# Long convolution and soft mixture of experts: the last eleven steps and the end as one list of stages

## The chip, the cores and the metric

The kernel runs on one core of a Trainium2 chip. Its engines work at the same time, each through its own queue in order: TensorE (PE; its weight loads are shown apart as PEld), VectorE (DVE), ScalarE (ACT), GpSimd (POOL), and SyncE (SP), which issues nearly all transfers. All numbers are float32. The metric is the device time of one execution in microseconds, as the median of the runs; lower is better.

## The reference

```python
Xf = np.fft.rfft(x, n=2 * S, axis=1)              # x: (8, 5696, 128), h: (5696, 128)
Hf = np.fft.rfft(h, n=2 * S, axis=0)
y = np.fft.irfft(Xf * Hf[None], n=2 * S, axis=1)[:, :S, :]
x = y.reshape(B * S, D)                           # 45568 tokens of 128
logits = x @ phi                                  # 32 slots, 8 experts of 4
d = np.exp(logits - logits.max(0)); d /= d.sum(0) + 1e-9      # over the tokens
slot_input = d.T @ x                              # (32, 128)
slot_out[e] = np.maximum(slot_input[e] @ w1[e], 0) @ w2[e]    # F = 1024
c = np.exp(logits - logits.max(1)); c /= c.sum(1) + 1e-9      # over the slots
return c @ slot_out
```

## The kernel before

The sequence of 5696 rows is seen as 89 rows of 64 columns, and the convolution is a transform in two stages forward, a product with the spectrum of h, and two stages back. A scratch in device memory lies between the stages. The work comes in three kinds.

- First stage, `stage_a(c, high)`: 72 chunks c (9 sequences, h first, of 8 chunks). `fold(c)` adds and subtracts mirrored columns on POOL (L216); the matmuls stand in L240, ACT takes the two banks out (L242), and two stores go to `fl` (the low columns, each chunk) or `fh` (the high ones, each second chunk, for two chunks at once).
- Middle, units u, 12 for each sequence, 0 to 107: `load_g(u)` loads from `fl` or `fh` (L272; three buffers). `stage_b1(u)` ("forward") multiplies on PE (L285) and then by the spectrum on DVE (L305 twice, L313 twice). `stage_b2(u)` ("backward") multiplies back (L328), ACT takes it out to `zst` (L333; three buffers), and the stores go to `zm` (two of 256 KB) for the first eight units of a sequence or to `zr` (four of 128 KB) for the rest. Forward u and backward u write the same one of two psum tiles, `bt` or `bz` by u % 2, so forward u + 2 waits until ACT has taken backward u out.
- Last stage and the layer of experts, pairs T, 4 for each sequence, 0 to 31: `load_main` and `load_rest` load `zc` (1024 KB) and `zx` (512 KB). `stage_c1` has two parts: the product (L413, L418, into four banks; ACT takes two out, L421 and L422; DVE adds and subtracts one, L405 and L406), and the sums (L405, L406 again, then four operations of L431 on POOL). Then `stage_c2` (turn: transposes, L440, L442), `stage_c3` (logits, L449, L454), `column_max` (L458 to L466), `stage_c4` (exponent: transposes of the logits, L476, L480, and the exponentials over tokens, L483, L487), `stage_c5` (tokens, L492, L495), `softmax_shift` (DVE L501, POOL L502), `softmax_exp` (ACT L508), `dispatch` (16 small matmuls, L533, and the sum on DVE, L538), `softmax_sum` (DVE L513 to L515), `softmax_scale` (POOL L520), and `stage_c6` (weights: transposes, L557; out to a scratch by L567 and L568, or in the end straight into `cT` by L562).

A store is not issued where it is made: it is put on `pending`, and `flush()` issues what is pending. A transfer on SP waits for its own data and for the buffer that it fills, and also for an earlier transfer, because completions share eight semaphores; whatever stands behind it on SP waits too. The banks of psum for everything except the units are four until the last unit is done and eight after that; which of them a stage gets is settled when the program is built.

A loop over 81 steps t sets the order. Up to step 71 each step has first-stage work: `low t` comes first in a step, `high` in each odd step behind the exponent; 1 or 2 units are done in a step (91 and 92 in step 70, 93 in 71, 94 and 95 in 72, and so on to 106 and 107 in step 80), each forward followed by the backward of the unit before it; product and sums of pair T come in step 2T + 27, right behind `low t` while there is one, exponent to exp of pair T in step 2T + 29, dispatch to scale of T in step 2T + 30, turn to maximum in step 2T + 28, weights in step 2T + 32. From step 73 on one of the eight `w1` is loaded at the end of each step (L737).

Behind the loop `front` is closed, which frees the memory of the units, and a list of words, `order`, sets the order of what is left: pairs 27 to 31, the placing of the weights that were put in the scratch (`place`, POOL L578; `cl`, L573), the loads of `w2` (L774), the experts (`inputs`, `hidden`, `flip`, `second`, `outputs`, L794 to L854). Last come the output matmuls (L908), their copies on DVE and ACT (L914, L916) and the stores (L924, L929).

Of the kernel before, what the change touches and what calls it, by code (L numbers as in the profile page):

```python
# [75 lines left out]
def kernel(  # L76
# [145 lines left out]
    def flush():  # L222
        while pending:
            pending.pop(0)()  # L224
# [390 lines left out]
    last_front = queue[-1][1]  # L615
# [19 lines left out]
    for t in range(last_front + 1):  # L635
# [13 lines left out]
        def slot_b(between=lambda: None):  # L649
# [6 lines left out]
            between()  # L656
# [4 lines left out]
        if t < NA:  # L661
            stage_a(t, False)
            fold(t + 1)
        if t == last_front:
            assert T is None and U is None
            assert pair(-1) % NQ
            flush()
            dispatch(W)
            for i in range(3):
                slot_b()  # L670
                flush()
                if i == 1:
                    softmax_sum(W)
                    softmax_scale(W)
                    stage_c2(V)
            assert not us and not wait_b2
            stage_c6(X)
            stage_c3(V)
            column_max(V)
            break  # L680
        if t % 2:
# [7 lines left out]
            if t < NA:  # L689
                slot_b()  # L690
                if U is not None:
                    stage_c4(U)
                stage_a(t, True)
            else:
                slot_b(lambda: stage_c4(U))
# [5 lines left out]
        else:  # L701
            if t % NJ == 0:
                prefetch(wait_b2[-1] + AHEAD if wait_b2 else AHEAD - 1)
            if t < NA:
                load_x(t // 2 + 2)
# [3 lines left out]
            if t < NA:  # L709
                slot_b()  # L710
                if W is not None:
                    softmax_sum(W)
                    softmax_scale(W)
                    dispatch(W)
                flush()
                if V is not None:
                    stage_c2(V)
                if X is not None:
                    stage_c6(X)
                slot_b()  # L720
            else:
                dispatch(W)
                slot_b()
                softmax_sum(W)
                softmax_scale(W)
                stage_c2(V)
                slot_b(lambda: stage_c6(X))
# [233 lines left out]
```

## Time and profile before

| what | value |
|---|---|
| time, median of 3 runs | 838.8 us (835.96 to 839.89) |
| the profiled execution's own time | 839.15 us |
| its span, first to last instruction | 837.4 us |
| mean granted TensorE clock | 0.955 |
| PE busy | 731.3 us (87%) |
| PEld busy | 361.2 us (43%) |
| DVE busy | 595.6 us (71%) |
| ACT busy | 424.6 us (51%) |
| POOL busy | 410.8 us (49%) |
| moved by the transfers | 282.48 MB, mean 337 GB/s |

The busy times are shares of the whole span, over stretches with different limits. For this change one stretch matters: the list begins where `low` of chunk 70 starts on PE, 601.02 us from the start of the span, and ends where the output matmuls start, at 772.38. What follows that, 65 us of output, holds the same instructions before and after.

In the rows of a timeline the first number is the start in us from the start of the span, the second how long the row lasted, then engine, line, operation, the tiles, how many instructions were merged, and in square brackets how long the engine had been idle before it and what ended that. In rows of a list of stretches each engine has its busy time and in brackets its instructions, then the granted clock, the busy share of the 16 transfer engines, and GB/s.

### The profile page before, as it was taken

How to read it: one execution, taken by the hardware profiler on the slowest of the kernel's cores; microseconds unless marked ns; L12 is line 12 of the kernel's file. 1: busy time of each engine (PE TensorE's matmuls, PEld its weight loads, DVE VectorE, ACT ScalarE, POOL GpSimd, SP SyncE). 2: the span in 40 equal slices, each digit the busy share in tenths (PEclk: the TensorE clock that was granted, in tenths of full speed). 3: DMA queues.
4: the chain of work that ended last, by engine and by line, in shares of the span. 5: the costliest groups of instructions: out<-in, count | busy, mean ns of one | idle time of the engine just before them, and what ended most of it. 6: DMA issues, size and time to landing. Idle time of an engine off the chain costs nothing.

```text
span 837.4 us, 21166 instructions
## 1 busy us (share of the span) xinstructions
PE 731.3 (87%) x8308; PEld 361.2 (43%) x8308; DVE 595.6 (71%) x895; ACT 424.6 (51%) x868; POOL 410.8 (49%) x368
## 2 busy tenths in 40 slices
PE   5868788779999999999999999999998887888893
PEld 1222233234444444444444444444444444455783
DVE  0039877747877877777788788777888996794642
ACT  2423344435655555566566555555664544564541
POOL 5634424235665555555555655565533353676000
PEclk9989999989999999999999999999999998999755
DMA  8999999999999999999999999999998995773998
GB/s 291 365 340 372 336 338 358 323 351 398 352 321 371 374 352 330 371 361 349 328 383 360 343 340 370 369 328 342 385 324 258 386 358 192 280 276 103 374 401 341
DMA packets 169707, 282.48 MB, mean 337 GB/s; under 512 B 13352, under 2 KB 132776, under 8 KB 164392
## 3 DMA queue, kind: packets, MB, share of 16 engines
q1 hardware_dynamic: 168600, 280.03, 95.0%
q8 instruction: 66, 1.08, 0.5%
q10 hardware_dynamic: 1008, 1.10, 0.4%
q14 instruction: 33, 0.27, 0.1%
HBM read 148.54 MB, written 132.53 MB: 336 GB/s over the span
## 4 chain that ended last, share of the span: by engine, by line
PE 40%; DMA 27%; ACT 9%; DVE 8%; POOL 6%; issue 4%; SPq 3%; ACTq 0%; DVEq 0%; POOLq 0%
PE bank L240 10%; PE bt L285 6%; DMA zx<-zr 6%; PE bank L413 5%; PE bz L328 5%; DMA zr<-zst 5%; POOL y L431 5%; DMA out_dram<-o 4%; PE bank L418 3%; DMA gt<-fl 3%; ACT zst L333 3%; ACT fst L242 3%; PE bank L449 2%; SPq L224 2%; DMA zm<-zst 2%
## 5 line engine op out<-in xcount | busy, mean ns | idle before, releaser
L240 PE MATMUL bank<-x,s 128*32 128x512 f32 (+1 forms) x1152 | 217.5, 613 | 10.8 <-POOL x L216 8.6
L216 POOL TENSOR_TENSOR x<-xc 128x512 f32<-128x512 f32 x144 | 180.4, 1278 | 88.4 <-PE bank L240 77.3
L431 POOL TENSOR_TENSOR y<-y,op 128x512 f32<-128x512 f32 x64 | 78.2, 1221 | 193.6 <-DVE op L405 191.0
L242 ACT ACTIVATE fst<-bank 128x512 f32<-128x512 f32 x216 | 122.6, 593 | 75.9 <-PE bank L240 48.9
L305 DVE TENSOR_TENSOR pi<-bt,Hi 128x1024 f32<-128x1024 f32 x96 | 112.5, 1172 | 41.7 <-PE bt L285 40.9
L285 PE MATMUL bt<-gt,wt 64*64 64x256 f32 x1620 | 115.7, 394 | 26.8 <-DMA gt<-fl 10.6
L333 ACT ACTIVATE zst<-bz 128x1024 f32<-128x1024 f32 x96 | 93.2, 971 | 85.5 <-PE bz L328 61.1
L313 DVE TENSOR_TENSOR yf<-bt,pi 128x512 f32<-128x512 f32 x192 | 119.2, 662 | 3.3
L305 DVE TENSOR_TENSOR bt<-bt,Hr 128x1024 f32<-128x1024 f32 x96 | 113.0, 1177 | 0.0
L240 PEld LDWEIGHTS bank<-x,s 128*32 128x32 f32 (+1 forms) x1152 | 52.8, 124 | 128.1 <-issue 87.4
L328 PE MATMUL bz<-yf,vt 64*64 64x256 f32 x1440 | 101.7, 385 | 6.8 <-DVE yf L313 6.7
L285 PEld LDWEIGHTS bt<-gt,wt 64*64 64x64 f32 x1620 | 54.3, 134 | 103.6 <-issue 29.1
L405 DVE TENSOR_TENSOR y<-bank,y 128x512 f32<-128x512 f32 x32 | 22.1, 689 | 81.8 <-ACT y L421 81.8
L440 PE MATMUL bank<-ident,y 109*128 109x109 f32 x512 | 64.3, 268 | 17.3 <-ACT yt L442 14.9
L328 PEld LDWEIGHTS bz<-yf,vt 64*64 64x64 f32 x1440 | 55.7, 134 | 34.6 <-DVE yf L313 13.4
L508 ACT ACTIVATE L<-L 128x512 f32<-128x512 f32 x32 | 20.3, 634 | 91.9 <-POOL L L502 91.9
L440 PEld LDWEIGHTS bank<-ident,y 109*128 109x128 f32 x512 | 50.6, 144 | 34.4 <-POOL x L216 20.8
L431 POOL TENSOR_TENSOR y<-y,om 128x512 f32<-128x512 f32 x54 | 64.0, 1186 | 2.1
L520 POOL TENSOR_TENSOR L<-L,rs 128x512 f32<-128x512 f32 x32 | 33.6, 1050 | 61.2 <-DVE rs L515 37.2
L421 ACT ACTIVATE y<-bank 128x512 f32<-128x512 f32 x32 | 19.1, 597 | 79.4 <-PE bank L418 79.4
L413 PE MATMUL bank<-zc,im 64*64 64x512 f32 x480 | 58.5, 602 | 1.0 <-DMA zc<-zm 1.0
L442 ACT ACTIVATE yt<-bank 128x360 f32<-128x360 f32 x128 | 52.8, 485 | 4.8 <-PE bank L440 4.3
(99 smaller groups left out, 834.7 us busy)
## 6 DMA issues: line engine op xcount, KB each, us to landing
fl<-fst SPq DMA_DIRECT2D x144, 256.0 KB, 6.2
gt<-fl SPq DMA_DIRECT2D x72, 512.0 KB, 5.8
zm<-zst SPq DMA_DIRECT2D x128, 256.0 KB, 6.3
zc<-zm SPq DMA_DIRECT2D x30, 1024.0 KB, 8.3
fh<-fst SPq DMA_DIRECT2D x72, 256.0 KB, 7.3
xc<-in_x_dram SPq DMA_DIRECT2D x32, 512.0 KB
out_dram<-o SPq DMA_DIRECT2D x16, 1024.0 KB, 4.7
zx<-zr SPq DMA_DIRECT2D x30, 512.0 KB, 8.3
```

What stands on the lines that cost most here:

```text
L216: nc.gpsimd.tensor_tensor(out=y_[:, o, :, :], in0=near, in1=far, op=AL.subtract if o else AL.add)
L240: nc.tensor.matmul(p[i * m:(i + 1) * m, :], s1[:, q + o, cols], columns(c_, o), start=True, stop=True)
L242: nc.scalar.activation(st[:, :, q, :], p[:, :].rearrange("p (n d) -> p n d", d=D), AF.Copy)
L285: nc.tensor.matmul(bt[q * HP:(q + 1) * HP, a, o, :], wt[r, 2 * i + q, :], t_[r, 2 * o + q, :, :].rearrange("p c d -> p (c d)"), start=True ...
L305: nc.vector.tensor_tensor(out=p_, in0=pv, in1=h_, op=AL.mult)
L313: nc.vector.tensor_tensor(out=y_[r, 0:k, c, :], in0=pv[:, :, c, :], in1=pi[r, 0:k, 1 - c, :], op=op_)
L328: nc.tensor.matmul(bz[a * HP:(a + 1) * HP, q, o, :], vt[r, i, a, :], y_[r, a * m + o, :, :].rearrange("p c d -> p (c d)"), start=True, sto ...
L333: nc.scalar.activation(st[:, 0:m, 0:n, :].rearrange("p o q x -> p q o x"), bz[:, 0:n, 0:m, :], AF.Copy)
L413: nc.tensor.matmul(ps[o, c][h_ * HP:(h_ + 1) * HP, :], im[r, c, :], zt[r, h_, :, c, :], start=True, stop=False)
L431: eng.tensor_tensor(out=part_, in0=part(v, 0), in1=o_[:, :, :], op=sign)
L440: nc.tensor.transpose(p[:, i * TR:(i + 1) * TR], ys[T][0:TR, k * CH + i, 0:D], ident[0:TR, 0:TR])
L442: nc.scalar.activation(yt[:, k * CH:(k + 1) * CH, :, :], of_tokens(p), AF.Copy)
```

## The change

The loop now ends behind step 69. What steps 70 to 80 did, and what the old list `order` did, is written as one list of words that is run in three parts, because `lead` and `front`, pools of memory, are closed between them. Each word is a stage and its number: `low`, `high` and `fold` a chunk, `loadf`, `forward` and `backward` a unit, `load`, `loadz`, `loadr` and the words from `product` to `weights` a pair, `fetchv` one `w1`. The functions behind the words are the same as before; the stages done are the same ones, each once. `load 28`, which stood directly behind `front.close()`, and the last `w1` are words too. The way in which x is loaded (even partitions, and each fourth one) is the same in both.

Steps 70 to 80 before, written in the same words, and the list after, up to the end of the units:

```text
before
 70: low70 fold71 flush forward91 loadf94 backward90 rowsum20 scale20 dispatch20 flush turn21
     weights19 forward92 loadf95 backward91 logits21 maximum21 flush
 71: low71 product22 sums22 flush load23 forward93 backward92 exponent21 high71 tokens21 shift21
     exp21 flush
 72: loadf96 flush dispatch21 forward94 loadf97 backward93 rowsum21 scale21 turn22 forward95
     loadf98 weights20 backward94 logits22 maximum22 flush
 73: product23 sums23 flush loadz24 forward96 loadf99 exponent22 backward95 tokens22 shift22 exp22
     flush fetchv0
 74: loadr24 flush dispatch22 forward97 loadf100 backward96 rowsum22 scale22 turn23 forward98
     loadf101 weights21 backward97 logits23 maximum23 flush fetchv1
 75, 77, 79: product sums flush load forward loadf exponent backward tokens shift exp flush fetchv
 76, 78: dispatch forward loadf backward rowsum scale turn forward loadf weights backward logits
     maximum flush fetchv
 80: flush dispatch25 forward106 backward105 flush forward107 backward106 flush rowsum25 scale25
     turn26 backward107 flush weights24 logits26 maximum26
after
 "flush weights19 low70 fold71 backward90 flush forward91 rowsum20 scale20 dispatch20 "
 "flush turn21 loadf94 forward92 product22 loadf95 backward91 flush logits21 flush "
 "maximum21 sums22 load23 forward93 backward92 exponent21 low71 high71 tokens21 shift21 "
 "flush loadf96 flush forward94 loadf97 backward93 exp21 dispatch21 rowsum21 turn22 "
 "forward95 scale21 weights20 backward94 logits22 maximum22 flush product23 sums23 loadf98 "
 "forward96 backward95 flush loadz24 "
 "loadf99 exponent22 tokens22 shift22 exp22 fetchv0 flush loadr24 flush dispatch22 flush "
 "forward97 loadf100 backward96 rowsum22 turn23 forward98 loadf101 weights21 logits23 "
 "scale22 maximum23 flush backward97 fetchv1 product24 sums24 load25 forward99 exponent23 "
 "backward98 loadf102 flush shift23 tokens23 fetchv2 dispatch23 exp23 forward100 loadf103 "
 "backward99 rowsum23 turn24 forward101 loadf104 product25 backward100 logits24 maximum24 "
 "scale23 weights22 fetchv3 exponent24 sums25 flush load26 forward102 loadf105 backward101 "
 "tokens24 shift24 exp24 fetchv4 flush dispatch24 flush forward103 loadf106 flush "
 "backward102 rowsum24 scale24 turn25 forward104 weights23 flush loadf107 logits25 "
 "maximum25 fetchv5 product26 sums26 backward103 flush loadz27 exponent25 loadr27 flush "
 "forward105 backward104 tokens25 shift25 exp25 flush forward106 backward105 dispatch25 "
 "forward107 backward106 flush rowsum25 flush scale25 turn26 backward107 weights24 "
 "logits26 flush fetchv6 maximum26 "
```

The diff, cut to its core (in the old list `+0` is pair 27):

```diff
-    last_front = queue[-1][1]
+    END = NA - 2
...
-    for t in range(last_front + 1):
+    for t in range(END):
...
-        if t == NA:
-            lead.close()
-            wts = inner.enter_context(tc.tile_pool(name="wts", bufs=1, side="right"))
-            w1s = wts.tile([P, E, F], F32, name="w1s")
-        if NA < t <= NA + E:
-            nc.sync.dma_start(out=w1s[:, t - NA - 1, :], in_=moe_w1[t - NA - 1])
...
+    def run(words):
+        for word in words.split():
+            name, n = re.fullmatch(r"([a-z]+)(\d*)", word).groups()
+            stages[name](*[int(n)] if n else [])
...
+    lead.close()
+    wts = inner.enter_context(tc.tile_pool(name="wts", bufs=1, side="right"))
+    w1s = wts.tile([P, E, F], F32, name="w1s")
...
     front.close()
...
-    load_pair(V + 2)
-    nc.sync.dma_start(out=w1s[:, E - 1, :], in_=moe_w1[E - 1])
...
-    order = (
-        "spread product+0 weights-2 exponent-1 clear shift-1 sums+0 tokens-1 load+2 exp-1 fetch "
-        "fetch dispatch-1 rowsum-1 scale-1 turn+0 logits+0 maximum+0 exponent+0 shift+0 exp+0 "
-        "product+1 place2 sums+1 tokens+0 weights-1 dispatch+0 load+3 zero rowsum+0 scale+0 "
-        "place2 product+2 sums+2 load+4 turn+1 logits+1 product+3 maximum+1 turn+2 exponent+1 "
-        "tokens+1 shift+1 exp+1 sums+3 place2 dispatch+1 rowsum+1 logits+2 weights+0 fetchw0 "
-        "fetchw2 maximum+2 scale+1 exponent+2 shift+2 product+4 turn+3 place2 sums+4 tokens+2 "
-        "exp+2 weights+1 logits+3 dispatch+2 maximum+3 rowsum+2 place2 fetchw4 scale+2 turn+4 "
-        "exponent+3 fetchw6 shift+3 logits+4 tokens+3 exp+3 weights+2 place4 maximum+4 rowsum+3 "
-        "scale+3 exponent+4 dispatch+3 tokens+4 join dispatch+4 shift+4 weights+3 exp+4 inputs "
-        "rowsum+4 scale+4 place32 hidden0 hidden1 flip0 weights+4 flip1 second0 second1 outputs ")
+    run(
+        "load28 product27 exponent26 clear fetchv7 shift26 sums27 flush tokens26 spread weights25 "
+        "load29 exp26 fetch fetch dispatch26 flush rowsum26 turn27 logits27 maximum27 exponent27 "
+        "scale26 weights26 shift27 product28 tokens27 flush place2 sums28 exp27 loadz30 zero "
+        "loadr30 rowsum27 dispatch27 place2 product29 load31 flush turn28 scale27 logits28 sums29 "
+        "product30 maximum28 exponent28 turn29 tokens28 shift28 exp28 sums30 rowsum28 weights27 "
+        "logits29 fetchw0 fetchw2 scale28 maximum29 place2 dispatch28 exponent29 shift29 "
+        "product31 turn30 place2 sums31 tokens29 logits30 exp29 weights28 place2 rowsum29 fetchw4 "
+        "dispatch29 scale29 maximum30 turn31 exponent30 logits31 fetchw6 flush shift30 weights29 "
+        "tokens30 exp30 place4 maximum31 rowsum30 exponent31 dispatch30 tokens31 scale30 join "
+        "dispatch31 shift31 weights30 exp31 inputs rowsum31 scale31 place32 hidden0 hidden1 flip0 "
+        "flip1 second0 second1 weights31 outputs ")
```

More of the change, by code (lines that the diff above doesn't have):

```diff
@@ L660 @@
         T, U, V, W, X = [pair(k) for k in (0, 2, 1, 3, 5)]
[L661 to L680, printed above, removed]
+        stage_a(t, False)
+        fold(t + 1)
         if t % 2:
@@ L688 @@
                     load_rest(pair(-2))
[L689 to L695, printed above, removed]
+            slot_b()
+            if U is not None:
+                stage_c4(U)
+            stage_a(t, True)
             if U is not None:
@@ L753 @@
     y_ = tail["pool"].tile([P, Q * CH, D + 1], F32, name="y2", tag="y2", bufs=1)
[L755 removed]
+    landed = []
     def fetch_c():
@@ L854, in join_experts @@
         nc.vector.tensor_copy(out=so4[:, :], in_=p[:, 0:D])
[L855 to L859 removed]
+    stages.update(place=placed_c, fetchw=load_w2, clear=clear_y, spread=spread, fetch=fetch_c, join=join_quarters,
                   zero=zero_slots, inputs=expert_in, hidden=layer_1, flip=turn_h, second=layer_2,
                   outputs=join_experts)
[L862 removed]
[10 rows of a table removed]
[L873 to L879 removed]
+    run(
[11 rows of a table added]
+    assert not (Ls or ys or ds or prods or gs or zs or xs or folded or kept or landed or held)
     inner.close()
```

54 lines of the change are left out of this document (20 added, 34 removed), and 18 rows, old and new, of tables (scale, w1s).

## The prediction, made before the changed kernel ran

> **What bounds the kernel now.** I read the list of stretches first, to see which engine sets the end where, then the timeline of each stretch for the idle times in brackets.
>
> ```profile
> 600.00:620.00 20.00, 19.29 (x232) 9.38 (x228) 15.91 (x25) 11.72 (x25) 9.13 (x9) 1.00 1.01 347
> 620.00:640.00 20.00, 16.96 (x236) 8.97 (x232) 17.94 (x29) 10.09 (x24) 10.23 (x10) 1.00 0.87 279
> 640.00:660.00 20.00, 17.22 (x232) 9.60 (x232) 19.19 (x29) 10.52 (x21) 8.23 (x8) 1.00 0.93 332
> 700.00:720.00 20.00, 15.35 (x160) 8.13 (x156) 11.20 (x20) 10.96 (x33) 8.62 (x12) 0.91 0.82 311
> 772.00:837.00 65.00, 45.79 (x712) 42.35 (x712) 29.18 (x51) 24.44 (x50) 4.25 (x9) 0.64 0.93 361
> ```
>
> Up to 620 PE is the bound (19.29 of 20 us), with DVE idle for 4.1. From 640 on, without first-stage work, DVE is (19.19). From 700 on, nothing is: the one chain through PE, ACT, DVE and POOL is. From 772 on the stores run at 361 GB/s, and the order of that part is untouched, so it only starts earlier or later. No edit changes an operation; the sum is of idle times.
>
> **The first-stage steps (601 to 633): 0.3 us gained.** The list puts `product22` and `forward93` ahead of `low71`, so that DVE gets its sums sooner:
>
> ```profile
> 611.47 1.94 PE L240 MATMUL bank<-x,s 128*64 128x512 f32 x8
> 617.02 0.69 DVE L405 TENSOR_TENSOR y<-bank,y 128x512 f32<-128x512 f32 x1 [2.51 <-ACT y L421]
> 607.97 0.57 PE L440 MATMUL bank<-ident,y 109*128 109x109 f32 x4 [0.71 <-ACT yt L442]
> 622.05 1.09 PE L533 MATMUL bank<-y,d 128*32 128x129 f32 x32 [0.80 <-ACT d L495]
> 633.44 0.69 DVE L405 TENSOR_TENSOR y<-bank,y 128x512 f32<-128x512 f32 x1 [1.69 <-ACT y L421]
> ```
>
> The 2.51 us before the sums of pair 22 go. But at the next product DVE waits again (1.69 at 633.44), and that wait ends when PE has done the same work as before: between `low70` and `product23` the list holds the same stages. PE's own idle there is 0.71 + 0.80 = 1.51, so no more can be won. The list keeps the first (the fourth transpose still waits for the first copy), saves the second, and adds one: `forward93` needs `zst91`, which now stands on ACT behind the two copies of `product22`, about 0.5. I take 0.3, with bounds of 1.5 gained and 1.5 lost (the clearest loss, a late load, is the rival below). [...]
>
> **The steps on DVE (633 to 694): 0.95 us gained.** DVE's order is nearly the old one. In each pair it stands still once, for ACT's copy of the new product:
>
> ```profile
> 650.13 0.69 DVE L405 TENSOR_TENSOR y<-bank,y 128x512 f32<-128x512 f32 x1 [0.47 <-ACT y L421]
> 666.82 0.69 DVE L405 TENSOR_TENSOR y<-bank,y 128x512 f32<-128x512 f32 x1 [0.47 <-ACT y L421]
> 683.51 0.69 DVE L405 TENSOR_TENSOR y<-bank,y 128x512 f32<-128x512 f32 x1 [0.47 <-ACT y L421]
> 667.67 1.09 PE L328 MATMUL bz<-yf,vt 64*64 64x256 f32 x16
> ```
>
> `product24` keeps its place. `product25` and `product26` now stand before the backward (1.09 on PE, in the row at 667.67 a later one), so their copies come before DVE asks: 2 x 0.47 = 0.94. What stands behind them instead, the backward, has slack: its store's buffer is asked for three units later. Bounds: 0, if another wait takes the place, and 1.41 for all three.
>
> **The change-over (694 to 715): 0.75 us gained.**
>
> ```profile
> 703.40 0.59 PE L557 MATMUL bank<-ident,L 109*128 109x109 f32 x4
> 704.02 0.59 ACT L422 ACTIVATE om<-bank 128x512 f32<-128x512 f32 x1
> 704.85 0.66 ACT L562 ACTIVATE cT<-bank 128x90 f32<-128x90 f32 x4 [0.23 <-DMA zr<-zst]
> 705.36 0.63 ACT L480 ACTIVATE L<-bank 128x512 f32<-128x512 f32 x1
> 706.68 0.66 PE L492 MATMUL bank<-ident,dt 128*128 128x128 f32 x4 [2.25 <-ACT dt L483]
> ```
>
> Before, `weights25` stands between `product27` and `exponent26`, and its copies into `cT` (memory just freed) hold ACT until the last `zr` stores have landed. L480 stands behind them, then L483, then PE's `tokens26`, which waited 2.25. After, the exponent and the tokens come first. L480 then starts at about 704.6, when ACT's copies of the product end (L422, 704.02 + 0.59), instead of 705.36: 0.75, and the chain of dispatch and turn behind it follows. The wait for the stores moves to POOL's `clear`, with `shift26` behind it, which before stood behind `spread` on the same wait. Bounds 0 and 2.25.
>
> **The middle of the end (715 to 750): 0.8 us gained.**
>
> ```profile
> 731.21 1.60 ACT L442 ACTIVATE yt<-bank 128x360 f32<-128x360 f32 x4
> 732.72 0.60 ACT L480 ACTIVATE L<-bank 128x512 f32<-128x512 f32 x1
> 734.04 0.66 PE L492 MATMUL bank<-ident,dt 128*128 128x128 f32 x4 [1.36 <-ACT dt L483]
> 735.38 1.95 PE L533 MATMUL bank<-y,d 128*32 128x129 f32 x32 [0.69 <-ACT d L495]
> ```
>
> PE idles for 1.36 + 0.69 = 2.05 around pair 28. `exponent28` now comes before `turn29` on PE and ACT, and `dispatch28` behind `weights27` and `logits29`, so both waits have work under them. Against it, the four copies of the turn (1.60) now stand on ACT behind L480 (0.60) and the exponentials (about 0.8, as L492 starts 1.32 behind L480's start), so `logits29` can wait up to 1.4 longer for them; but it used to stand behind the dispatch (1.95), which has gone behind it. And `turn28`'s last bank waits for `dispatch27`'s sum, which stands behind the three row sums of pair 27 on DVE, about 1.1. 2.05 - 1.1 = 0.95, of which I take 0.8. Bounds: 2.05 gained, 1.6 lost.
>
> **The last stages: 0.4 us gained.**
>
> ```profile
> 766.05 0.54 PE L557 MATMUL bank<-ident,L 109*128 109x109 f32 x4
> 767.39 3.70 PE L841 MATMUL bank<-w2s,zc 128*32 128x128 f32 x128
> 771.16 0.29 DVE L850 COPY so<-bank 128x128 f32<-128x128 f32 x1 [2.97 <-PE bank L841]
> ```
>
> `weights31` leaves the chain in front of the second layer (0.4 of its 0.54, as transposes start before the last ends) and runs while DVE copies the result (0.29). Its copies into `cT` are needed only by the last batch and by the small tile for the odd row. Bounds 0 and 0.54.
>
> **The clock: 1.4 us gained.**
>
> ```profile
> 692.00:694.00 2.00, 0.65 (x4) 0.20 (x4) 1.97 (x3) 1.14 (x2) 0.00 (x0) 1.00 0.42 161
> 694.00:696.00 2.00, 1.66 (x16) 0.78 (x16) 1.86 (x4) 0.00 (x0) 0.00 (x0) 0.61 0.59 169
> 696.00:700.00 4.00, 4.00 (x32) 3.04 (x32) 1.48 (x5) 3.19 (x7) 1.05 (x1) 0.77 0.30 84
> 708.00:712.00 4.00, 3.98 (x46) 3.53 (x47) 3.93 (x5) 1.42 (x3) 2.56 (x2) 0.57 0.95 358
> 732.00:736.00 4.00, 1.95 (x23) 1.45 (x25) 3.62 (x8) 3.20 (x9) 1.89 (x2) 0.93 0.99 371
> 736.00:740.00 4.00, 3.98 (x48) 2.39 (x43) 3.93 (x5) 1.26 (x7) 3.92 (x4) 0.65 1.00 405
> ```
>
> Each time that PE has idled for 2 us or so (1.35 of 692 to 694, the 2.25 before 706.68, 2.05 of 732 to 736), the granted clock is low for the next 3 to 4. The time lost is busy time by what is missing of the clock: 1.66 x 0.39 + 4.00 x 0.23 = 1.57 behind 693, 3.98 x 0.43 = 1.71 behind 707, 3.98 x 0.35 = 1.39 behind 735; together 4.7. The idle at 734 is the one that the list breaks up most, so I take its 1.4; the one at 707 shrinks less, and the first is only split in two. Bounds 4.7 gained and, for one new spell, 1.5 lost. [...]
>
> **The sum.** 0.3 + 0.95 + 0.75 + 0.8 + 0.4 + 1.4 = 4.6. The profiled execution took 839.15 us (1.75 of it outside its span of 837.4), 0.35 above the median of the runs and inside their range. 839.15 - 4.6 = 834.55; taken from the median it would be 834.2. I forecast 834.3.
>
> **The rivals.** (1) Slower: SP's queue. Where a waiting transfer stands ahead, all behind it is late.
>
> ```profile
> 614.08 1.24 SPq L224 DMA_DIRECT2D fl<-fst x2
> 623.64 4.07 SPq L272 DMA_DIRECT2D gt<-fl x3
> 666.71 0.33 SPq L375 DMA_DIRECT2D zc<-zm x1
> fl<-fst SPq DMA_DIRECT2D x144, 256.0 KB, 6.2
> gt<-fl SPq DMA_DIRECT2D x72, 512.0 KB, 5.8
> gt<-fh SPq DMA_DIRECT2D x27, 512.0 KB, 8.9
> zc<-zm SPq DMA_DIRECT2D x30, 1024.0 KB, 8.3
> ```
>
> `loadf96` must wait for the stores of `low71`. These were issued at 614.08, 9.6 us ahead of it; after, `low71` stands about 6 us later on PE and the stores directly ahead of the load, at about 621 to 622. So it goes out at 622 + 6.2 = 628.2, lands at 634.0, and `forward96` is wanted at about 632. PE waits 1.8; DVE, busy with pair 23 until about 635.9 (four of 0.69 from 633.44, less 0.3), does not feel it up to 0.8 more. If loads there take 8.9, it is 3.1 more and costs 2.3 net, and `loadz24` and all stores behind it slip too. The same again at `loadz26`: the scratch store of `weights22` (now done behind `product25`) stands ahead of it and of two units' stores, so it goes out at about 670 instead of 666.71, with 8.2 left for its 8.3; 3.1 more costs about 2.3. Then the first three terms (2.0) are lost too, with some 1 us for the last loads: 839.15 + 2.3 + 2.3 + 1 + (4.6 - 2.0 taken off) = 842.2, and 846.8 when both spots cost twice that. It decides from landings of about 6.6 us on. For it: the transfer engines are busy for 0.87 to 1.01 of these stretches. Against it: no product of steps 640 to 690 waited for its load. (2) No difference: DVE's work from 633 to 694 and the chains of the end are the same ones, each wait that goes is followed by another, and only the forced parts stay: half of 0.95, 0.75 and 0.4, about 1 us; 838. For it: DVE's order barely changes. (3) More: two of the cold spells go, or all: 834.3 - 1.57 - 1.71 = 831.0. (4) That the change does nothing is out: in the built program the engines' queues stand in the new order from chunk 70 on.
>
> **The numbers.** The forecast (832.6 to 836.5) 0.40, the slower case 0.20, no difference 0.23, more 0.17. A difference under 0.5% (4.2 us, 834.6 to 843.0) is about what cannot be told from none. Faster: somewhat over half of the forecast, all of (3): 0.41. Slower: the upper part of (1): 0.14, with a little for what I have not seen, 0.17. Within: 0.42. The range leaves out about 0.1 at each end: 829.5 to 843.0.
>
> **What would show it.** `sA` of pairs 25 and 26 (L405) without the 0.47; DVE's wait before pair 23's at 1.2 to 1.7; L480 of pair 26 within 1.1 us of the end of `product27`'s last matmul; granted clock over 0.9 where `dispatch28` runs; `weights31` behind the last L841. The distance from `low70` to the output's first matmul, 171.36 before (601.02 to 772.38), should be about 166.8. I am wrong if PE waits for `gt` before `forward96` by over 2.5 us, if `product24` or `product26` waits for `zc`, or if new cold spells stand where PE idled between `forward106` and `forward107`.

## The result, and the profile after

| kernel | median of runs | ratio to the kernel before, 95% interval |
|---|---|---|
| before, beside the changed kernel | 838.29 us (834.05 to 843.93, 20 executions) | |
| changed | 834.94 us (830.3 to 840.2, 20 executions) | 0.9955 [0.9936, 0.9973] |
| changed, a second comparison | 836.92 us (833.91 to 842.74, 12) | 0.9996 [0.9971, 1.0020] |
| before against itself | 839.23 us (835.31 to 844.34, 12) | 1.0003 [0.9973, 1.0033] |

The changed kernel is a little faster: 0.45% in the first comparison, nothing to speak of in the second. Weighted by the inverse squares of the widths of their intervals the two give 0.9970 [0.9955, 0.9985], about 2.5 us; they lie farther apart than such intervals let one expect, so its size is known to 2 us only.

The profiled execution took 839.07 us (span 837.2). It is in the upper part of its 20: its list began 2.76 us later than before (603.78 against 601.02), behind 600 us in which no instruction was moved. So I measure from the start of the list (`weights19`, which now stands ahead of `low70`) to the output's first matmul. The timeline of PE in the changed kernel (start, length, and in brackets the idle time before and what ended it):

```profile
603.78 0.54 PE L557 MATMUL bank<-ident,L 109*128 109x109 f32 x4
...
682.32 1.95 PE L413 MATMUL bank<-zc,im 64*64 64x512 f32 x16 [0.56 <-DMA zc<-zm]
...
706.42 0.66 PE L492 MATMUL bank<-ident,dt 128*128 128x128 f32 x4 [1.75 <-ACT dt L483]
...
725.66 1.87 PE L440 MATMUL bank<-ident,y 109*128 109x109 f32 x16 [1.69 <-POOL y L431]
...
735.48 0.66 PE L492 MATMUL bank<-ident,dt 128*128 128x128 f32 x4 [1.59 <-ACT dt L483]
...
766.74 3.70 PE L839 MATMUL bank<-w2s,zd 128*32 128x128 f32 x128
770.37 0.59 PE L557 MATMUL bank<-ident,L 109*128 109x109 f32 x4
770.86 0.49 PE L850 MATMUL bank<-so,rep 128*128 128x128 f32 x2
771.82 1.52 PE L897 MATMUL op<-so,cT 32*128 32x128 f32 x29 [0.47 <-DVE so L852]
```

771.82 - 603.78 = 168.04, against 171.36: 3.32 gained, of 4.6 predicted. `weights31` (770.37) stands behind the second layer; the wait before pair 26's tokens (L492) fell from 2.25 to 1.75; and `turn28` (725.66) waits 1.69 us for POOL, a wait that was not there before. `tokens28` (735.48) still waits, 1.59 us where it was 1.36, and `product26` (682.32) waits 0.56 for its `zc`: a sign of being wrong that I had named. DVE's timeline, the sums of pairs 23 to 26 (the rows of L405 alone):

```profile
635.71 0.69 DVE L405 TENSOR_TENSOR y<-bank,y 128x512 f32<-128x512 f32 x1 [1.92 <-ACT y L421]
653.22 0.69 DVE L405 TENSOR_TENSOR y<-bank,y 128x512 f32<-128x512 f32 x1 [0.49 <-ACT y L421]
668.54 0.68 DVE L405 TENSOR_TENSOR y<-bank,y 128x512 f32<-128x512 f32 x1
671.04 0.69 DVE L405 TENSOR_TENSOR op<-bank,om 128x512 f32<-128x512 f32 x1 [0.27 <-PE bank L476]
...
686.00 0.69 DVE L405 TENSOR_TENSOR y<-bank,y 128x512 f32<-128x512 f32 x1
```

The waits of pairs 25 and 26 are gone, as predicted; a small one for a bank (0.27) is new. The list of stretches (PE's busy time first, then the granted clock as the third number from the end):

```profile
692.00:696.00 4.00, 2.44 (x52) 1.53 (x52) 3.96 (x6) 1.54 (x2) 2.01 (x2) 1.00 0.99 369
696.00:700.00 4.00, 3.76 (x42) 2.40 (x39) 3.73 (x9) 2.27 (x5) 0.02 (x1) 1.00 0.77 229
704.00:708.00 4.00, 1.94 (x28) 1.49 (x24) 3.17 (x5) 3.21 (x11) 1.27 (x3) 0.99 0.54 165
708.00:712.00 4.00, 3.91 (x47) 3.20 (x40) 3.93 (x5) 1.77 (x6) 3.81 (x5) 0.58 0.85 294
732.00:736.00 4.00, 2.41 (x25) 2.21 (x24) 3.36 (x8) 2.81 (x8) 1.67 (x2) 1.00 0.99 342
736.00:740.00 4.00, 3.63 (x57) 2.17 (x59) 3.93 (x4) 3.25 (x12) 3.12 (x3) 1.00 0.97 367
```

Of the three spells of a low clock, those behind 693 and 735 are gone; the one behind 706 stays. A new one stands at 640 (36 us from the start of the list).

### The profile page after: what moved, and what is told of

It reads as the page before. It is cut to its first block, busy times and chain, and to the rows that moved or that the text cites. A ratio compares the mean times of both kernels' runs of the same rounds, so it can differ in the third digit from the quotient of the medians.

```text
span 837.2 us, 21161 instructions
## 1 busy us (share of the span) xinstructions
PE 728.5 (87%) x8308; PEld 360.6 (43%) x8308; DVE 595.6 (71%) x895; ACT 425.9 (51%) x868; POOL 411.6 (49%) x368
## 4 chain that ended last, share of the span: by engine, by line
PE 41%; DMA 31%; DVE 10%; ACT 8%; SPq 3%; issue 3%; POOL 2%; ACTq 0%; DVEq 0%; POOLq 0%
PE bank L240 11%; DMA zx<-zr 9%; PE bt L285 7%; DMA zc<-zm 6%; PE bank L413 5%; PE bz L328 5%; DMA out_dram<-o 4%; PE bank L418 4%; DMA zr<-zst 3%; ACT fst L242 3%; DMA fl<-fst 3%; SPq L224 2%; ACT zst L333 2%; DMA gt<-fl 2%; DVE pi L305 2%
## 5 line engine op out<-in xcount | busy, mean ns | idle before, releaser
L405 DVE TENSOR_TENSOR y<-bank,y 128x512 f32<-128x512 f32 x32 | 22.1, 690 | 83.0 <-ACT y L421 83.0
L413 PE MATMUL bank<-zc,im 64*64 64x512 f32 x480 | 58.3, 601 | 1.3 <-DMA zc<-zm 1.3
```

Of the source, the lines that this page charges most:

```text
L413: nc.tensor.matmul(ps[o, c][h_ * HP:(h_ + 1) * HP, :], im[r, c, :], zt[r, h_, :, c, :], start=True, stop=False)
```

## The experiments

One profile of a kernel is one draw, so the table sets all of them side by side, cut where the same instruction can be found in each: the start of the list, the first sum (L405) of pair 24, that of pair 26, `tokens26` (L492), `product31` (L413), the output's first matmul. The last column tells where spells of a low clock began, in us from the start, by stretches of 2 us: the first one in which PE's busy time, times what was missing of the clock, was over 0.1 us. Each number is the difference of two rows of a timeline. The ratios in the text are to the kernel before, run beside each: `e1` to `e4` in one batch, `e5` to `e7` beside `a1_changed_again`, `e9` and `n2` beside `b1_before_again`, `n3` by itself, each batch on another chip.

| kernel | start to sums 24 | to sums 26 | to tokens26 | to product31 | to output | in all | low clock at |
|---|---|---|---|---|---|---|---|
| before | 49.11 | 33.38 | 23.17 | 33.14 | 32.56 | 171.36 | 92, 106, 134 |
| b1_before_again | 49.11 | 33.39 | 23.18 | 33.05 | 35.07 | 173.80 | 92, 106, 134, 158 |
| changed | 49.44 | 32.78 | 20.42 | 33.08 | 32.32 | 168.04 | 36, 104 |
| a1_changed_again | 49.66 | 32.78 | 20.42 | 36.17 | 32.34 | 171.37 | 36, 104, 124 |
| e1_steps_only | 50.22 | 32.65 | 22.50 | 35.74 | 35.07 | 176.18 | 106, 126, 136, 160 |
| e2_end_only | 49.12 | 33.38 | 25.20 | 34.43 | 32.35 | 174.48 | 92 (to 103), 112 |
| e3_place_behind | 49.59 | 32.98 | 20.42 | 32.67 | 32.35 | 168.01 | none |
| e4_exponent22_first | 50.66 | 32.65 | 20.42 | 34.98 | 32.30 | 171.01 | 108 |
| e5_loads_later | 49.87 | 32.65 | 20.42 | 31.77 | 32.34 | 167.05 | 88, 102 |
| e6_loads_and_chain | 49.51 | 32.64 | 19.31 | 35.00 | 33.14 | 169.60 | 88, 106 |
| e7_weights25_front | 49.25 | 32.65 | 22.78 | 33.40 | 32.34 | 170.42 | 36, 104 |
| e9_load24_first | 49.17 | 32.64 | 20.42 | 34.71 | 32.33 | 169.27 | 102, 122 |
| n2_all | 48.75 | 32.64 | 20.41 | 31.17 | 33.14 | 166.11 | 102 |
| n3_exponentials_first | 49.25 | 32.64 | 19.93 | 33.20 | 33.78 | 168.80 | 36, 106 |

Most columns repeat to 0.1 us wherever the same words stand there. What scatters is the first column, the spells, and the stretch from `tokens26` to `product31`.

**The two kernels once more.** No edit.

> The changed kernel itself, unaltered, for a second profiled execution. Theory: which of PE's idle times of about 2 us is followed by a low clock differs from one execution to the next, since the kernel without weights moved (the one with only the end's two placings behind) showed none at pair 22 though its list is the same there; so the spell at 640 to 644 is absent or another one appears, and the distance from low70 (with weights19) to the output's first matmul differs from 168.04 us by 1 us or more in either direction. Rival: the spells belong to the order: the same ones at the same places and a distance of 167.6 to 168.5. In both cases the ratio is 0.9940 to 0.9975.

> The kernel before itself, unaltered, for a second profiled execution and for what a comparison of a kernel with itself gives here. Theory: the waits that set off a low clock are the order's, the places where it then falls are partly chance, so of the three spells of the first profile (92, 106 and 134 us behind low70) one or two come again, the distance from low70 to the output's first matmul lies within 3 us of 171.36, and the ratio within 0.997 to 1.003. Rival: the spells come again at the same three places and the distance is 171.0 to 171.8.

The changed kernel took 171.37 where its first profile took 168.04, and its ratio, 0.9996, is above what I expected in either case. Nearly all of that, 3.09, lies between `tokens26` and `product31`. About 1.0 of it comes at `turn27`, which waited for POOL:

```profile
705.79 3.17 PE L440 MATMUL bank<-ident,y 109*128 109x109 f32 x16 [1.06 <-POOL y L431]
```

POOL's first operation in this place, `clear` (L776), does not start before the last `zr` stores have landed, and `shift26` and the sums of pair 27 stand behind it. It came 1.33 behind the start of `tokens26` here (703.04 and 701.71), and 0.06 ahead of it in the first profile. POOL's timeline in `e3`, where the wait for POOL before `turn27` is 1.07, names the stores:

```profile
702.48 0.12 POOL L776 MEMSET y<- 128x16 f32 x1 [6.13 <-DMA zr<-zst]
```

In every profile POOL's first operation behind these stores starts 1.5 us behind the end of their last issue (also in the two of the changed kernel, where the row names ACT as the releaser), 102.2 to 104.2 behind the start of the list; it is 103.9 in the three profiles with the old steps. Of the rest, 0.7 lies at `turn27` and the logits behind it, where the spell at 104 lasted longer (6.8 us at 0.50, and 3.4 in the first profile), and 1.3 at `turn28`: POOL came 1.95 late for it instead of 1.69, and a new spell stood behind it (124). The kernel before shows its three spells again at the same places, and a fourth at 158, which cost 2.5. That one stands in two of the three profiles with the old end (`e1` too, at 160) and in none of the eleven with the new. So the places mostly belong to the order, and which of them is taken differs from one execution to the next (the one at 36 stands in four of ten profiles with the same words, the last section); by the means of two profiles each, 172.6 and 169.7, the change wins 2.9.

**Half of the change at a time.** `e1` has the old end behind the new steps, `e2` the new end behind the old steps:

```diff
 e1   run("... logits26 flush fetchv6 maximum26 ")        # new
-     run("load28 product27 exponent26 clear fetchv7 shift26 sums27 flush tokens26 spread weights25 ...
+     run("load28 fetchv7 spread product27 weights25 exponent26 clear shift26 sums27 tokens26 load29 ...
 e2   the words of steps 70 to 80 before, then the new third list
```

> New order from step 70 to the end of the units, old order for pairs 27 to 31 and the end. Measure: the distance from low70's first matmul to the output's first matmul (171.36 us before, 168.04 after). Theory: the new trace is 2.15 us ahead at product27, most of it because the cold spell of the clock behind step 80 is gone; that lead is kept by the old end, so the distance is 169.0 to 169.7, the ratio to the kernel before about 0.9975. Rival: the old end's weights25 waits on ACT for the last zr stores, which are as late as ever, so the lead is lost at the change-over: 170.8 to 171.4, ratio 0.9990 to 1.0005.

> Old order for steps 70 to 80, new order for what stands behind. Theory: the end by itself wins what the change-over (about 0.9) and weights31 (0.3) won and loses nothing in the middle: 170.0 to 170.4 for the distance, ratio about 0.9985; the cold spell behind step 80 (694 to 700 before) stays, that of 736 to 740 goes. Rival: with the cold spell behind step 80 back, the exponent of pair 26 is late as well and the change-over wins nothing: 171.0 to 171.5. A result under 169.5 would say that the end won most of the change.

The ratios are 0.9983 [0.9957, 1.0008] and 0.9972 [0.9948, 0.9996]; multiplied they give 0.9955, the whole change's in the first comparison, so the times don't show that the halves need each other. What follows rests on the traces. In `e1` the lead is there at `product27`, which starts 97.96 behind the start of the list (696.06 - 598.10) and did so 99.46 behind it before. At `tokens26` it is gone: 105.37 and 105.66. ACT's timeline in `e1`:

```profile
699.60 0.59 ACT L422 ACTIVATE om<-bank 128x512 f32<-128x512 f32 x1
701.64 0.66 ACT L562 ACTIVATE cT<-bank 128x90 f32<-128x90 f32 x4 [1.45 <-DMA zr<-zst]
702.15 0.63 ACT L480 ACTIVATE L<-bank 128x512 f32<-128x512 f32 x1
702.63 0.79 ACT L483 ACTIVATE dt<-lt,low 128x352 f32<-128x352 f32 x2
```

ACT stands for 1.45 until the last `zr` stores have landed, with L480 and L483 queued behind it: the rival's mechanism. (The distance, 176.18, is longer than the rival's: the spells at 126, 136 and 160, and 1.72 of waiting for `zx` of pair 24.) In `e2` (174.48) neither of my numbers came. The clock stayed at about half behind the old steps' last units, and `tokens26` came 2.03 later behind the sums of pair 26 than before:

```profile
692.00:702.00 10.00, 10.00 (x64) 5.18 (x56) 3.52 (x10) 4.18 (x9) 1.05 (x1) 0.53 0.40 115
```

So neither half shows the whole's 2.75 at `tokens26` by itself: `e1` has 0.67 of it, and in `e2` the long spell hides what there may be.

**The change-over alone.**

```diff
-  load28 product27 exponent26 clear fetchv7 shift26 sums27 flush tokens26 spread weights25
+  load28 spread product27 weights25 exponent26 clear fetchv7 shift26 sums27 flush tokens26
```

> The changed kernel with weights25 between product27 and exponent26, and the small copies of the identity first on POOL, as before. It prices the change-over alone, with the new steps in front. Theory: weights25's copies hold ACT until the last zr stores have landed, pair 26's exponentials stand behind them, and PE's wait before tokens26 grows from 1.75 to 3.2 to 3.8 us: the distance grows by 1.5 to 2.5 to 169.5 to 170.5, ratio 0.9965 to 0.9985. Rival: as predicted, the wait costs 0.75 or less: 168.0 to 168.8, ratio 0.995 to 0.9965.

```profile
706.95 1.11 PE L492 MATMUL bank<-ident,dt 128*128 128x128 f32 x4 [3.74 <-ACT dt L483]
```

PE's timeline: 3.74, as the theory had it, and the third column grows by 2.36 (22.78 against 20.42). Ratio 0.9982 [0.9955, 1.0008]. Behind the new steps the new order is worth 2.1 (`e1`) to 2.4 (`e7`) at `tokens26`, not the 0.75 that I had read from the old trace. One stage on, counted from POOL's first operation behind the stores, `turn27` starts 5.0 to 5.5 us behind it with `weights25` in front (`before`, `b1`, `e1`, `e7`) and 2.3 to 3.2 with `exponent26` in front (nine profiles). The times don't show it: beside the changed kernel's 836.92 `e7` took 837.25, a third of a microsecond more.

**The wait on POOL.** First where it comes from. SP's timeline, the kernel before and then the changed one:

```profile
689.40 0.60 SPq L737 DMA_DIRECT2D w1s<-in_moe_w_dram  x1
...
707.29 0.97 SPq L573 DMA_DIRECT2D cl<-c_t  x2
```

```profile
704.93 0.58 SPq L705 DMA_DIRECT2D w1s<-in_moe_w_dram  x1
...
708.64 2.20 SPq L573 DMA_DIRECT2D cl<-c_t  x2
```

and POOL's, again before and after:

```profile
718.45 1.74 POOL L578 COPY cT<-cl 128x360 f32<-128x360 f32 x2 [0.82 <-DMA cl<-c_t]
```

```profile
721.88 2.58 POOL L578 COPY cT<-cl 128x360 f32<-128x360 f32 x2 [4.36 <-DMA cl<-c_t]
724.43 2.45 POOL L431 TENSOR_TENSOR y<-y,op 128x512 f32<-128x512 f32 x2
```

`fetchv6` (the `w1s` row) went out 18 us ahead of the load of the scratch before; now its 512 KB stand in the same burst, behind the last stores. The load lands 13.2 us after its issue (708.64 to 721.88) where it took 11.2 (707.29 to 718.45). The placing waits for it on POOL, and the sums of pair 28, for which DVE is ready, stand behind the placing. In the old trace the same order was hidden, as the load had landed 1.7 us before the sums could start (DVE's op at 720.13). In the seven profiles that have `fetchv6` in the burst and show this wait the load takes 13.0 to 14.8, in both profiles of the kernel before 11.2. No run moves `fetchv6` alone, so that its bytes make the difference, and not the order of the stores ahead of it, is argued and not shown.

```diff
 e3
-  place2 sums28
+  sums28 place2
 e5, beside e3
-  ... clear fetchv7 shift26 ... exp26 fetch fetch dispatch26 ... loadr30 rowsum27 ... load31 flush
+  ... clear shift26 ... exp26 fetch dispatch26 ... loadr30 fetch rowsum27 ... load31 fetchv6 fetchv7 flush
```

> The changed kernel with the first two placings moved behind the sums of pair 28 on POOL (nothing else). Theory: POOL's sums of pair 28 no longer stand behind the wait for the scratch's load (idle 4.36 us to 721.88 in the changed kernel), PE's wait of 1.69 us before turn28 is under 0.4, and the distance falls from 168.04 to 166.4 to 167.0, ratio about 0.9940. Rival: the placing, 2.6 us of POOL, then stands in front of the scale of pair 27 and the sums of pair 29, and the wait comes back there: 167.7 to 168.4, ratio 0.9950 to 0.9960.

> The first two placings behind the sums of pair 28, the last two loads of w1 behind the last load of a pair, and the second load of the scratch behind the load of pair 30. Theory: with PE's wait on POOL gone, the load of pair 30 bounds the middle of the end (PE waited 0.85 us for it in the kernel with the placings behind, the transfers being at 1.0 from 712 to 724); with 1.7 MB less in front of it at some 0.42 MB per us it lands up to 3 us earlier, product30 starts 0.85 to 1.3 earlier, and the distance is 166.5 to 167.3; ratio 0.990 to 0.994. Rival: the chain of pair 28's exponent and the tokens behind it sets the end whatever the loads do: 167.7 to 168.4.

In `e3` the wait before `turn28` is gone (`turn28` at 719.36), but PE then stands for the next load:

```profile
719.36 1.34 PE L440 MATMUL bank<-ident,y 109*128 109x109 f32 x12
...
723.73 1.95 PE L413 MATMUL bank<-zd,im 64*64 64x512 f32 x16 [0.85 <-DMA zd<-zm]
```

so the distance, 168.01, is the rival's, for another reason than the rival gave: this wait, the 1.07 before `turn27`, and 1.09 for `zx` of pair 24. Its ratio, of 6 executions, is better than either side had. With the bytes in front taken away (`e5`) `product30` comes 21.09 behind `tokens26` (721.48 - 700.39) instead of 22.00, the stretch falls to 31.77, and the distance to 167.05, inside the theory's range. Ratios 0.9913 [0.9885, 0.9942] and 0.9953 [0.9927, 0.9979]; the medians beside each other are 833.4 for `e5` and 836.9 for the changed kernel. The spell at 122 to 128, seen in three of the kernels with the placing in front, is in none of the five that have it behind.

**The other two waits of the end.**

```diff
 e6, beside e5
-  load28 product27 exponent26 ...   sums29 product30 maximum28 exponent28
+  load28 exponent26 product27 ...   sums29 maximum28 product30 exponent28
 n3, beside n2: in stage_c4 of pairs 26 to 31, L483 ahead of L480
```

> The kernel before this one, with two more words moved: exponent26 ahead of product27 (PE waits 1.75 us for pair 26's exponentials in every kernel with the new end), and maximum28 ahead of product30 on DVE (ACT waits 1.20 us for pair 28's maximum). Theory: both waits fall under 0.6 us, the low clock behind the first of them goes or halves, and the distance falls by another 2 to 3.5 us: 163.5 to 165; ratio 0.985 to 0.990. Rival: product27 stands 0.9 later on PE, so DVE's sums of pair 27 and POOL's behind them are later by that and turn27 waits for them: no more than 0.5 beyond the kernel with the loads alone.

> The kernel with all edits that won, and in stage_c4 of pairs 26 to 31 the two exponentials over tokens (L483) ahead of the copy of the logits (L480) on ACT. It prices the wait that no order of the stages removed: PE's 1.75 us before tokens26, in which ACT does the product's two copies, L480 and L483 in that order. Theory: with L480's 0.5 out of the chain, PE's waits before the tokens of pairs 26 and 31 fall by about 0.5 each, to 1.25 and 0.14, those of the other pairs stay hidden; DVE's L501 is 0.7 later each time and has room; the distance falls by 0.5 to 1.2 below 166.1. Rival: L501, late, holds the sums behind it on DVE and POOL's L502, and the waits come back before the next turn: 166 to 167. A difference of 1 us is too small for the ratio to settle (0.992 to 0.998 either way); the waits and the distance decide.

Both shorten the wait that they aim at (`tokens26` without one in `e6`, 1.27 in `n3`) and both lose it at once; before the tokens of pair 31 it stays (0.64 and 0.67). PE's timeline in `e6`, then in `n3`, where these lines of code have moved down by 3 to 5:

```profile
706.16 1.71 PE L440 MATMUL bank<-ident,y 109*128 109x109 f32 x8 [2.30 <-POOL y L431]
```

```profile
702.71 0.66 PE L497 MATMUL bank<-ident,dt 128*128 128x128 f32 x4 [1.27 <-ACT dt L486]
...
706.24 1.20 PE L440 MATMUL bank<-ident,y 109*128 109x109 f32 x8 [1.10 <-POOL y L431]
708.47 1.69 PE L440 MATMUL bank<-ident,y 109*128 109x109 f32 x8 [1.02 <-DVE y L431]
```

`turn27` needs the sums on POOL and DVE, which did not come earlier. On POOL they stand behind `clear` and so behind the last `zr` stores: `clear` came 1.95 behind the start of `tokens26` in `e6` and 1.12 in `n3`. The distances, 169.60 and 168.80, are beyond what I had expected on either side. `maximum28` ahead of `product30` wins 0.6 in one stretch and costs 0.8 in the next (31.17 and 33.14 in `n2` against 31.77 and 32.34 in `e5`). Ratios 0.9972 [0.9947, 0.9997] and 0.9933 [0.9900, 0.9965].

**The first column.**

```diff
 e4
-  forward96 backward95 flush loadz24 loadf99 exponent22
+  forward96 flush loadz24 loadf99 exponent22 backward95
 e9
-  product23 sums23 loadf98 forward96 backward95 flush loadz24
+  product23 sums23 loadf98 loadz24 forward96 backward95 flush
```

> The changed kernel with exponent22 ahead of backward95, as it was before. Theory: PE's waits for the exponentials and the tokens of pair 22 (1.36 and 0.69 us) have backward95 under them again, the granted clock stays over 0.95 where dispatch22 runs (0.61 at 640 to 644 in the changed kernel), DVE's wait of 0.71 before unit 97 goes, and unit 98's first DVE multiply comes 0.7 to 0.9 earlier; the end gains 0.3 to 0.9: 167.2 to 167.7. Rival: the stores of backward95, now later, put off the load of zx for pair 24, which PE already waits for (0.36 us): that wait grows by as much and nothing is left at the sums of pair 24: 167.9 to 168.5.

> The changed kernel with the main load of pair 24 ahead of forward96, as before, and not behind the stores of backward95. Theory: the load was issued 37.5 us behind the start of the list instead of 34.3 before, and PE's product24 waits for the zx load queued behind it in every profile of the new list (0.2 to 2.2 us), which is where the first stage's half microsecond is lost. Issued about 3 us earlier, the wait of L418 of pair 24 for zx falls under 0.4 and DVE's sums of pair 24 start 0.4 to 0.7 earlier (48.7 to 49.1 us behind the start, against 49.3 to 50.6); the end is lower by 0.5 at most, ratio 0.994 to 0.998. Rival: the zx load waits for the stores of backward95 anyway and for the bytes in front of it, and the sums of pair 24 stay at 49.3 to 50.6.

SP's timeline: the kernel before, the changed one, `e9`.

```profile
635.30 0.55 SPq L375 DMA_DIRECT2D zc<-zm  x1
642.62 0.33 SPq L386 DMA_DIRECT2D zx<-zr  x1
```

```profile
641.29 0.53 SPq L375 DMA_DIRECT2D zc<-zm  x1
642.95 0.54 SPq L386 DMA_DIRECT2D zx<-zr  x1
```

```profile
633.57 0.39 SPq L375 DMA_DIRECT2D zc<-zm  x1
640.40 0.32 SPq L386 DMA_DIRECT2D zx<-zr  x1
```

From each start, `zc` of pair 24 was issued at 34.28 before, 37.51 in the changed kernel (behind the stores of `backward95`) and 34.92 in `e9`. Issued late, its 1024 KB are in front of `zx`, for which PE then waits. `e4` makes that worse, as its rival said (its distance, 171.01, is beyond both ranges, with a spell of 6.8 us at 108 besides):

```profile
650.87 1.12 PE L418 MATMUL bank<-zx,ir 26*64 26x512 f32 x16 [2.15 <-DMA zx<-zr]
```

With `e9` the wait is 0.66 and the first column 49.17, both a little over what I expected. In `n2`, where a `w1` no longer stands ahead of `zx` either, they are 0.24 and 48.75. In the seven profiles of new steps without the spell at 36 the first column is PE's wait for `zx` and 48.51, to 0.01 us (from 0.24 and 48.75 to 2.15 and 50.66). So the new order without that wait is 0.6 ahead of the 49.11 before, and the wait takes most of it back, or more. In the four profiles with that spell another 0.4 to 1.2 comes on top; `a1` and `e7` have no wait for `zx` at all. Ratios 0.9966 [0.9943, 0.9990] and 0.9989 [0.9959, 1.0019].

**All that won.** `n2` is `e5` with `maximum28` ahead of `product30`, `loadz24` as in `e9`, `fetchv0` behind `loadr24` and `fetchv3` behind `load26`. `e9` ran in the same batch, so the move of `loadz24` had not won yet, and those of `fetchv0` and `fetchv3` have no run of their own.

> All edits that won in a profile, together: the loads of w1 behind the loads of pairs 24, 26 and 31, the main load of pair 24 ahead of forward96, the first two placings behind the sums of pair 28, the second load of the scratch behind the load of pair 30, and maximum28 ahead of product30 on DVE. Theory: the sums of pair 24 start under 49.2, PE's wait before turn28 is gone, product30 does not wait for zd, ACT's wait for pair 28's maximum is under 0.3; together 2 to 4 us less than the changed kernel in the distance: 164.5 to 167, and with the spread of the clock spells a ratio of 0.988 to 0.9945. Rival: the spells of the clock and the chain through DVE and POOL give it back: ratio 0.995 to 0.998, no better than the changed kernel.

The distance is 166.11, the shortest of all, inside the theory's range; the ratio is 0.9953 [0.9928, 0.9977], in the rival's. It beats the kernel before. The five kernels with the placings behind lie at 0.9913 to 0.9972, the changed kernel at 0.9955 and 0.9996: that they beat it is likely for `e3`, `e5`, `n2` and `n3`, but the intervals overlap, so it isn't settled. By the table `e5` with the first column of `n2` would be the best, 48.75 + 32.65 + 20.42 + 31.77 + 32.34 = 165.9; that wasn't tried.

## Why the prediction was right

The median of the first comparison is 0.6 us from the forecast of 834.3. Both medians lie in the range (829.5 to 843.0), the second just above the forecast's own band (832.6 to 836.5); by the pooled ratio the gain is 2.5 us, between the forecast (4.5) and the rival of no difference (1). That the sum came near is partly luck, as its terms show, each against the first profile of before:

| term | predicted | first profile | second profile |
|---|---|---|---|
| first-stage steps (to sums 24) | 0.3 | -0.33 | -0.55 |
| steps on DVE (sums 24 to sums 26) | 0.95 | 0.60 | 0.60 |
| change-over (to tokens26) | 0.75 | 2.75 | 2.75 |
| middle and the clock (to product31) | 0.8 + 1.4 | 0.06 | -3.03 |
| last stages (to the output) | 0.4 | 0.24 | 0.22 |
| in all | 4.6 | 3.32 | -0.01 |

- First-stage steps. Pair 23's sums came 0.49 earlier (31.93 behind the start instead of 32.42) and the wait before them was 1.92, over my 1.2 to 1.7. The order gave 0.6, twice my 0.3; the step that failed is what I did not cost. `loadz24` moved past the stores of `backward95`, so `zx` came late for `product24` (0.36 in the first profile, nothing in the second). And a new spell at 36, which goes with the rest (0.57 and 1.15), stands behind waits of 1.36 and 0.69 us that `backward95`, now ahead of `exponent22`, no longer shortens. I had named SP's queue as a rival, but at `loadf96` and `loadz26`. There PE waited 0.8 at most for `gt` (in `a1`) and for `zc` of pair 26 (in `e3`; 0.56 in the changed kernel), of which DVE felt 0.25.
- Steps on DVE: the mechanism was right; 0.60 and not 0.95, as DVE now waits 0.27 for a bank in the sums of pair 25.
- Change-over: the mechanism was right (L480 starts 1.04 behind the end of `product27`, at 705.11), the term mis-sized, and by more than its upper bound of 2.25. I priced it with the old arrival of `product27`. The stores land about where they did; with the steps as they now are, ACT is ready earlier, so the old order would have cost 3.74 of waiting (`e7`). I had seen that the wait moves to `clear` on POOL but gave it no price: in the second profile it takes 1.0 back at `turn27`. And the spell at 92, which I counted as "only split in two", went: PE's wait before `forward107` fell from 2.20 to 1.18, and the spell is in all three profiles of the old steps and, some 4 us earlier, in two of eleven of the new.
- Middle: the size was right where I looked and the term failed ahead of it. From `turn28` to `product31` it is 13.84 us instead of 16.08 (725.66 to 739.50, 723.74 to 739.82), 2.24 gained against 0.8 + 1.4. The wait before `dispatch28` went and the spell at 134 with it (in three of three profiles with the old end, in none of eleven with the new). The wait before `tokens28` did not: PE stands 1.59 there, though `turn29` is now under it, as ACT waits 1.20 for pair 28's maximum. From `tokens26` to `turn28` 2.18 was lost, 1.69 of it PE's wait for POOL at `turn28`, which comes from the late load of the scratch and the placing (in `e3`, with the placing behind, it is gone). The second profile lost 4.17 there, 1.0 of it at `turn27`, and paid a new spell behind `turn28`.
- Last stages: from the first matmul of the hidden layer to the output 10.83 before (761.55 to 772.38) and 10.62 after (761.20 to 771.82). `weights31` keeps PE until 770.86, so the matmul that needs DVE's copy starts a little late: half of the 0.4.

## What to carry to other kernels

Where a wait ends with a transfer that stays where it is, price the edits in front of it and the edit that takes it away together: in `e1` a lead of 1.5 us at `product27` was 0.3 at `tokens26`. Then ask who waits for that transfer next; here it was POOL. For each load that moves, list what now stands behind it in the same burst and which in-order queue waits on that one. And where waits of PE like those here, of 1.36 to 2.25 us, are followed by a clock of 0.50 in one profile and not in the next, take two profiles of each kernel before believing a difference of 3 us.

## What the runs showed of the hardware

The same idle time is followed by a low clock in one execution and not in another. The list of stretches, 1 us each, around `dispatch22` in the changed kernel:

```profile
637.00:638.00 1.00, 0.25 (x3) 0.01 (x1) 0.96 (x3) 0.81 (x3) 0.20 (x1) 1.00 0.78 221
638.00:639.00 1.00, 0.39 (x4) 0.39 (x4) 1.00 (x2) 0.65 (x3) 0.98 (x1) 1.00 0.75 217
639.00:640.00 1.00, 0.31 (x7) 0.07 (x9) 1.00 (x2) 0.60 (x1) 0.94 (x1) 0.84 0.90 154
640.00:641.00 1.00, 1.00 (x20) 0.92 (x24) 0.96 (x2) 0.00 (x0) 1.00 (x2) 0.50 0.84 303
641.00:642.00 1.00, 1.00 (x24) 0.57 (x18) 1.00 (x3) 0.00 (x0) 0.92 (x2) 0.50 0.75 248
642.00:643.00 1.00, 1.00 (x12) 0.63 (x16) 0.89 (x3) 0.00 (x0) 0.94 (x2) 0.50 0.75 125
643.00:644.00 1.00, 1.00 (x21) 0.57 (x16) 0.40 (x1) 0.21 (x1) 0.76 (x1) 0.96 0.79 295
```

and at the same place in `e3`, with the same words there:

```profile
632.00:633.00 1.00, 0.01 (x1) 0.00 (x0) 0.96 (x3) 0.96 (x2) 0.24 (x1) 1.00 1.08 314
633.00:634.00 1.00, 0.64 (x4) 0.42 (x4) 1.00 (x2) 0.40 (x3) 0.94 (x1) 1.00 0.56 160
634.00:635.00 1.00, 0.32 (x13) 0.29 (x16) 1.00 (x2) 0.60 (x1) 0.99 (x1) 1.00 0.74 103
635.00:636.00 1.00, 1.00 (x37) 0.74 (x28) 0.96 (x2) 0.00 (x0) 1.00 (x2) 1.00 0.84 314
```

PE was busy for 0.95 of 3 us in the one and for 0.97 in the other. In the one the clock is then 0.50 for 3.4 us (the rows miss 0.16 + 3 x 0.50 + 0.04 us of clock), in the other it stays at 1.00. Of the ten profiles of kernels that kept PE's words there four show it (36 in the table). In the changed kernel's words it cost nothing in the end: the first column is 49.25 to 49.66 with it and 49.51 to 50.22 without, where PE waited 1.00 to 1.72 for `zx`. Where `zx` comes sooner it did cost: `n3` has 49.25 with the spell, `n2` 48.75 without, with the same words. Ahead of `dispatch22` PE waited 1.36 us (before `tokens22`) and 0.69 in both.

The lists of stretches, 2 us each, also tell how long the spells last. There are 30 in the list of words in the fourteen profiles, at a clock of 0.50: 22 miss 1.70 to 1.72 us of clock, which is 3.4 us at 0.50, seven miss 3.40 to 3.42 (6.8 us), and one, in `e2`, 5.12 (10.2 us). In the kernel before they start at 694.46, 708.11 and 735.42, behind waits of PE of 2.20 and 0.50, of 2.25 and 0.69, and of 1.36 and 0.69 us. So an order sets where PE has its pauses; which of them a low clock follows differs from execution to execution, and what decides that, no run here shows.

Nor does a spell always cost what it takes from PE. In the whole stretch of `e3` the clock was granted in full, and its 168.01 is no shorter than the 168.04 of the changed kernel with two spells, since PE waited for loads in it (1.09, 0.76, 0.24 and 0.85) and 1.07 for POOL; the spell at 158 in `b1`, where nothing but the one chain runs, cost 2.5.
